# Windowed attention with a feed-forward layer: TensorE in the order of the program, one weight piece per step

## The chip, the cores and the metric

The kernel runs on one core of a Trainium2 chip. The metric is the time of one execution on the device in microseconds (us), the median of several runs. TensorE (PE) multiplies, VectorE (DVE), ScalarE (ACT) and GpSimd (POOL) work on elements, SyncE (SP) issues most of the transfers. PEld is TensorE's loading of the stationary operand.

## What is computed

Eight batches, eight heads, 576 positions of 64 numbers. Four heads attend to the last 32 positions, four to every fourth of the last 128. The result, as 4608 rows of 512, goes through a feed-forward layer with a hidden width of 2048.

```python
    scores = scale * np.matmul(q, k.transpose(0, 1, 3, 2))
    scores = np.where(masks[None, :, :, :], scores, -1000000000.0)
    attn = softmax(scores)                      # written out in the reference
    x = np.matmul(attn, v)  # as (4608, 512)
    h = x @ w_in                                # 512 -> 2048
    g = h * np.clip(h + 3.0, 0.0, 6.0) / 6.0
    out = g @ w_out                             # 2048 -> 512
```

## The kernel before, in words

**Attention.** 48 "trios" `t` hold a sixth of a batch's query blocks each. For a trio `st_both` issues 48 small score matmuls (L163) and, between them, 48 small value matmuls (L173 or L181) of an earlier trio: one block. For the first 12 trios (`NFIRST`) a mask matmul (L228) stands ahead. `softmax` is two DVE operations (L195, L196; three for the later trios) and one exponential on ACT (L200). `normalise` is three on DVE (L207, L208, L210). The first 12 trios are transposed on PE (`turn`, L242; ACT copies the result, L245 for the attention weights `a`, L247 for the output `xf`), the later 36 on DVE with four small transfers (`turn_by_blocks`). `st_split` writes `xf` as a rounded part `xh` (ACT, L299) and a rest `xl` (POOL, L302), the input of the feed-forward layer.

**Feed-forward.** 12 chunks `c` of 384 rows, 16 slices `f` of the hidden width: 192 steps `(c, f)`. `gemm1` of a step is 12 matmuls of 384 columns (L407 to L409); ACT and DVE turn them into `gh` and `gl` (L412, L413, L416, L417); `gemm2`, two steps later (`LAG`), is 9 matmuls of 512 columns (L428 to L430). The order of the steps is (0,0) to (0,3), then (0,4), (1,0), (0,5), (1,1) and so on, then chunk after chunk.

**Weights.** They come in 32 pieces (piece 2f is slice f of `w_in`, piece 2f+1 of `w_out`). `convert_beat` moves each piece through three stages, one stage a beat: `cv_fields` (two ACT operations L338, L339, one DVE L340), `cv_join` (DVE L346, L350, ACT L351), `cv_split` (DVE L355). A beat also issues the loads of pieces up to three ahead (`load_ahead`, on SP). 32 pieces need 34 beats.

**Order.** The start is a loop over `tau` from 0 to 15: `first_items(tau)` traces the block of trio `tau` (scores) and `tau-3` (values), the transpose of the weights of trio `tau-1`, the transpose and split of trio `tau-4`; then come the beats of `CB` (14, two each for tau 6 to 12) and the steps of `EARLY` (step 0 at tau 8, ... step 7 and 8 at tau 15). The other steps follow. `step_at(n)` traces `gemm1` of step n, pieces of attention from `beside`, a beat, `gemm2` of step n-2, more of `beside`, and, for even n from 4 to 28, another beat. The program's order isn't the order of issue: every instruction carries a priority (`turn_of`), and a scheduler orders each engine's queue by priority and by the times that it simulates. `turn_of` gives `first_items(tau)` and `gemm1` of step tau-8 the same number. Within a queue the order is fixed at compile time, and each engine works it off in that order. `pace` ties the loads and two of the ACT operations of a piece behind the last PE instruction traced, in that scheduler's order.

Two PSUM pools matter: `ps_h` (2 buffers, `gemm1`) and `ps_a` (6 buffers: blocks, transposes, and three for the output of each open chunk).

Of the kernel before, what the change touches and what calls it, by code (L numbers as in the profile page):

```python
# [23 lines left out]
SPARE = 2  # L24
WORK = 12
BEATS = 30
EXTRA = 2
WARM = 8
ONV = ()
AHEAD = 3  # L30
LEAD = 4
# [15 lines left out]
def windowed_attention_ffn(ctx: ExitStack, tc: tile.TileContext, qk, vp, w, mask, out):  # L47
# [286 lines left out]
    def cv_fields(p):  # L334
        if p % 2 == 0:
            wt[p // 2] = wpool.tile([P, 4, WN], F32R, name="wt", tag="w")
        hi_w, lo_w, v, a, _, _ = parts(p)
        pace(nc.scalar.mul(v, hi_w, 2.0**-112))  # L338
        pace(nc.scalar.mul(a.bitcast(U32), lo_w.bitcast(U32), 2.0**-29))  # L339
        nc.vector.tensor_scalar(  # L340
            out=v.bitcast(U32), in0=v.bitcast(U32), scalar1=3, scalar2=None, op0=ALU.logical_shift_left
        )

    def cv_join(p):
        hi_w, _, v, a, hi, _ = parts(p)
        nc.vector.scalar_tensor_tensor(  # L346
            out=v.bitcast(U32), in0=hi_w.bitcast(U32), scalar=0x80000000, in1=v.bitcast(U32),
            op0=ALU.bitwise_and, op1=ALU.bitwise_or,
        )
        nc.vector.tensor_tensor(out=v.bitcast(U32), in0=v.bitcast(U32), in1=a.bitcast(U32), op=ALU.add)  # L350
        nc.scalar.copy(hi, v)  # L351

    def cv_split(p):
        _, _, v, _, hi, lo = parts(p)
        nc.vector.tensor_tensor(out=lo, in0=v, in1=hi.bitcast(F32), op=ALU.subtract)  # L355
        del staged[p]
# [5 lines left out]
    def load_ahead(n):  # L362
        while beat["loaded"] < min(n, NP):
            f = beat["fields"] // 2
            if len(staged) + f + 1 + 1 > NF + SPARE and len(staged) > 0 and beat["loaded"] >= 2:
                break
            load_w(beat["loaded"])
            beat["loaded"] += 1

    def convert_beat():  # L370
        if beat["split"] < beat["join"]:
            cv_split(beat["split"])
            beat["split"] += 1
        if beat["join"] < beat["fields"]:
            cv_join(beat["join"])
            beat["join"] += 1
        p = beat["fields"]
        if p < NP:
            load_ahead(p + 1)
            if p < beat["loaded"]:  # L380
                cv_fields(p)
                beat["fields"] += 1
        load_ahead(p + AHEAD)
# [10 lines left out]
    def turn_of(n):  # L394
        tc.cur_priority = max(first[0] + int(n * STEP), 0) + 1000

    def gemm1(n, c, f):
        last["g"] = True
        weights_ready(f)
        assert all(x in written for x in trios if c in chunks(*x))  # L400
        read[c] += 1
        r0 = (c * CH) % (2 * S)
        ph = ps_h.tile([P, CH], F32, name="ps_h")
        for kt in range(NK):
            a, b = xh[:, kt, r0 : r0 + CH], xl[:, kt, r0 : r0 + CH]
            ks = slice(kt * P, (kt + 1) * P)
            nc.tensor.matmul(ph, lhsT=wt[f][:, 0, ks], rhs=a, start=(kt == 0), stop=False)  # L407
            nc.tensor.matmul(ph, lhsT=wt[f][:, 0, ks], rhs=b, start=False, stop=False)  # L408
            last["pe"] = nc.tensor.matmul(ph, lhsT=wt[f][:, 1, ks], rhs=a, start=False, stop=(kt == NK - 1))  # L409
        turn_of(n + EV)  # L410
        t = work_tile("t")
        nc.scalar.activation(t, ph, AF.Relu, bias=three, scale=1.0)  # L412
        nc.vector.scalar_tensor_tensor(out=t, in0=t, scalar=6.0, in1=ph, op0=ALU.min, op1=ALU.mult)  # L413
        gh = work_tile("gh", F32R)
        gl = work_tile("gl", F32R)
        nc.scalar.copy(gh, t)  # L416
        nc.vector.tensor_tensor(out=gl, in0=t, in1=gh.bitcast(F32), op=ALU.subtract)  # L417
        gs[c, f] = gh, gl

    def gemm2(c, f):  # L420
        gh, gl = gs.pop((c, f))
        if f == 0:
            po[c] = [ps_a.tile([P, DM], F32, name="ps_o", tag="ps_a") for _ in range(TT)]
        if f == NF - 1:
            o = wpool.tile([P, TT, DM], F32, name="o", tag="w")
        for tt in range(TT):
            ts = slice(tt * P, (tt + 1) * P)
            nc.tensor.matmul(po[c][tt], lhsT=gh[:, ts], rhs=wt[f][:, 2], start=(f == 0), stop=False)  # L428
            nc.tensor.matmul(po[c][tt], lhsT=gh[:, ts], rhs=wt[f][:, 3], start=False, stop=False)  # L429
            last["pe"] = nc.tensor.matmul(po[c][tt], lhsT=gl[:, ts], rhs=wt[f][:, 2], start=False, stop=(f == NF - 1))  # L430
            if f == NF - 1:
                nc.scalar.mul(o[:, tt], po[c][tt], 1.0 / 6.0)
                r = c * CH + tt * P
                nc.scalar.dma_start(out=out[r : r + P, :], in_=o[:, tt])
# [40 lines left out]
    def step_at(n):  # L475
        c, f = steps[n] if n < len(steps) else (None, None)
        turn_of(n)
        if c is not None:
            gemm1(n, c, f)
        turn_of(n + DEL)  # L480
        for step in beside.get((c, f, 0), []):
            step()
        turn_of(n + 0.4)
        if LEAD <= n < BEATS:
            convert_beat()
        turn_of(n + G2)
        if n >= LAG:
            gemm2(*steps[n - LAG])
        turn_of(n + DEL + 0.5)
        for step in beside.get((c, f, 1), []):  # L490
            step()
        turn_of(n + 0.9)
        if LEAD <= n < BEATS and n % EXTRA == 0:
            convert_beat()

    first[0] = BASE * STEP
    some = P + 2 * CH
# [12 lines left out]
    n = 0  # L510
    for tau in range(NFIRST + 4):
        turn_of(tau - BASE)
        first_items(tau)
        turn_of(tau - BASE + CD)
        for _ in range(CB.count(tau)):
            convert_beat()
        for _ in range(EARLY.count(tau)):
            step_at(n)
            n += 1
    while n < len(steps) + LAG:  # L520
        step_at(n)
        n += 1
# [92 lines left out]
```

## Time and profile before

| | us |
|---|---|
| median of 3 runs (lowest to highest) | 915.77 (915.74 to 917.31) |
| the profiled execution | 915.34 |
| its span | 913.6 |
| PE busy, PEld busy | 891.0, 791.6 |
| DVE, ACT, POOL busy | 444.0, 346.5, 62.5 |

The span is what the profiler sees between the first and the last instruction; 1.74 us of the execution's time lie around it. The page gives busy shares over the whole span and in 40 slices of 22.84 us; a stretch is read with the views by window and in order of time. The end of a matmul is modelled, and matmuls overlap, so what one costs in a sequence is the distance from its start to the start of the next.

### The profile page before, as it was taken

What the parts mean: (1) busy time and instruction counts of PE and PEld (TensorE: products, weight loads), DVE (VectorE), ACT (ScalarE), POOL (GpSimd) and SP (SyncE); (2) the same over time, 40 slices, a digit from 0 to 9 for tenths busy, and PEclk for the clock granted to TensorE, in tenths of its full rate; (3) what the DMA queues carried; (4) which work ended last, traced back from release to release, by engine and by line L of the source; (5) the groups of instructions that cost most, each with busy time, mean ns of one, the idle gap of its engine ahead of it and who ended that gap; (6) DMA issues with size and microseconds to landing.
All of it is one profiled execution on the core that took longest, in us unless ns stands there. A gap on an engine that the chain in (4) does not pass through costs nothing.

```text
span 913.6 us, 20574 instructions
## 1 busy us (share of the span) xinstructions
PE 891.0 (98%) x8732; PEld 791.6 (87%) x8732; DVE 444.0 (49%) x934; ACT 346.5 (38%) x661; POOL 62.5 (7%) x77
## 2 busy tenths in 40 slices
PE   6897999999999999999999999999999999999998
PEld 4576999989889899899888989988888998899996
DVE  3899983244545454444454445445444544422221
ACT  2778862333333333233333223233333332332322
POOL 0212100000010110000000000000100010000000
PEclk9799999999999999999999999999999999999999
DMA  9927430022313222222122123113211310100000
GB/s 354 386 83 260 140 93 0 1 95 89 86 54 119 72 70 81 66 67 84 47 85 85 48 64 104 51 46 99 71 49 52 116 32 11 45 5 1 36 1 34
DMA packets 37820, 74.87 MB, mean 82 GB/s; under 512 B 7264, under 2 KB 16608, under 8 KB 37728
## 3 DMA queue, kind: packets, MB, share of 16 engines
q1 hardware_dynamic: 32544, 64.12, 21.8%
q10 hardware_dynamic: 5184, 9.44, 2.7%
q8 instruction: 68, 1.11, 0.5%
q14 instruction: 24, 0.20, 0.1%
HBM read 57.02 MB, written 9.44 MB: 73 GB/s over the span
## 4 chain that ended last, share of the span: by engine, by line
PE 92%; DMA 4%; DVE 2%; ACT 1%; issue 0%; SPq 0%; POOL 0%
PE ps_o L428 15%; PE ps_h L407 15%; PE ps_h L409 14%; PE ps_h L408 14%; PE ps_o L429 14%; PE ps_o L430 14%; PE ps_a L181 3%; PE ps_a L163 2%; DMA first<-in_v 2%; DMA st<-in_w 1%; DMA v<-in_v 1%; DVE st L350 1%; DVE st L346 1%; DVE wt L355 0%; PE ps_a L242 0%
## 5 line engine op out<-in xcount | busy, mean ns | idle before, releaser
L413 DVE SCALAR_TENSOR_TENSOR t<-t,ps_h 128x384 f32<-128x384 f32 x192 | 106.3, 554 | 326.0 <-ACT t L412 325.8
L407 PE MATMUL ps_h<-xh,wt 128*128 128x384 f32 x768 | 261.5, 341 | 2.9 <-DVE t L413 2.8
L408 PE MATMUL ps_h<-xl,wt 128*128 128x384 f32 x768 | 259.9, 338 | 0.5 <-POOL xl L302 0.5
L409 PE MATMUL ps_h<-xh,wt 128*128 128x384 f32 x768 | 259.9, 338 | 0.0
L428 PE MATMUL ps_o<-wt,gh 128*128 128x512 f32 x576 | 228.7, 397 | 2.0 <-ACT gh L416 2.0
L429 PE MATMUL ps_o<-wt,gh 128*128 128x512 f32 x576 | 224.9, 390 | 0.0
L430 PE MATMUL ps_o<-wt,gl 128*128 128x512 f32 x576 | 221.3, 391 | 0.6 <-DVE gl L417 0.6
L412 ACT ACTIVATE t<-ps_h,three 128x384 f32<-128x384 f32 x192 | 111.1, 579 | 273.3 <-PE ps_h L409 273.0
L417 DVE TENSOR_TENSOR gl<-t,gh 128x384 fp32r<-128x384 f32 x192 | 107.0, 557 | 101.4 <-ACT gh L416 100.1
L407 PEld LDWEIGHTS ps_h<-xh,wt 128*128 128x128 f32 x768 | 144.9, 189 | 11.8 <-DVE t L413 3.3
L408 PEld LDWEIGHTS ps_h<-xl,wt 128*128 128x128 f32 x768 | 144.9, 189 | 8.7 <-POOL xl L302 0.6
L409 PEld LDWEIGHTS ps_h<-xh,wt 128*128 128x128 f32 x768 | 145.0, 189 | 0.8 <-issue 0.3
L416 ACT CAST gh<-t 128x384 fp32r<-128x384 f32 x192 | 98.5, 513 | 111.3 <-DVE t L413 109.1
L430 PEld LDWEIGHTS ps_o<-wt,gl 128*128 128x128 f32 x576 | 108.2, 188 | 24.2 <-DVE gl L417 1.0
L428 PEld LDWEIGHTS ps_o<-wt,gh 128*128 128x128 f32 x576 | 108.3, 188 | 20.1 <-ACT gh L416 2.3
L429 PEld LDWEIGHTS ps_o<-wt,gh 128*128 128x128 f32 x576 | 108.4, 188 | 15.7
L302 POOL TENSOR_TENSOR xl<-xf,xh 128x384 fp32r<-128x384 f32 (+3 forms) x72 | 62.2, 877 | 740.6 <-ACT xh L299 671.8
L200 ACT ACTIVATE e<-e 128x384 f32<-128x384 f32 x48 | 25.2, 526 | 112.4 <-DVE e L196 112.3
L163 PE MATMUL ps_a<-kq 64*32 64x64 f32 x1872 | 47.1, 225 | 0.0
L299 ACT CAST xh<-xf 128x384 fp32r<-128x384 f32 (+3 forms) x72 | 33.7, 536 | 34.7 <-DMA xf<-xf_t 34.6
L181 PEld LDWEIGHTS ps_a<-v,a 64*32 64x32 f32 x1728 | 35.8, 105 | 9.2 <-issue 8.6
L181 PE MATMUL ps_a<-v,a 64*32 64x65 f32 x1728 | 41.6, 225 | 0.0
(45 smaller groups left out, 494.6 us busy)
## 6 DMA issues: line engine op xcount, KB each, us to landing
st<-in_w SPq DMA_DIRECT2D x32, 512.0 KB, 5.7
kq<-in_qk SPq DMA_DIRECT2D x39, 416.0 KB, 4.5
v<-in_v SPq DMA_DIRECT2D x39, 390.0 KB, 3.5
out<-o ACTq DMA_DIRECT2D x36, 256.0 KB, 2.9
first<-in_qk SPq DMA_DIRECT2D x9, 416.0 KB, 8.0
first<-in_v SPq DMA_DIRECT2D x9, 390.0 KB, 8.5
a<-a_t SPq DMA_DIRECT2D x144, 24.0 KB, 1.8
xf<-xf_t SPq DMA_DIRECT2D x144, 24.0 KB, 1.8
```

The costliest lines, as they stand in the source:

```text
L163: last["pe"] = nc.tensor.matmul(ps[at : at + QB, 2 * QB * i : 2 * QB * (i + 1)], lhsT=x[rows, KW + QB * n : KW + QB * (n + 1)], rhs=x[rows ...
L181: last["pe"] = nc.tensor.matmul(ps[at : at + QB, i * W : (i + 1) * W], lhsT=ats[t][rows, QB * n : QB * (n + 1)], rhs=vs[t][rows, n, :], st ...
L407: nc.tensor.matmul(ph, lhsT=wt[f][:, 0, ks], rhs=a, start=(kt == 0), stop=False)
L408: nc.tensor.matmul(ph, lhsT=wt[f][:, 0, ks], rhs=b, start=False, stop=False)
L409: last["pe"] = nc.tensor.matmul(ph, lhsT=wt[f][:, 1, ks], rhs=a, start=False, stop=(kt == NK - 1))
L412: nc.scalar.activation(t, ph, AF.Relu, bias=three, scale=1.0)
L413: nc.vector.scalar_tensor_tensor(out=t, in0=t, scalar=6.0, in1=ph, op0=ALU.min, op1=ALU.mult)
L416: nc.scalar.copy(gh, t)
L417: nc.vector.tensor_tensor(out=gl, in0=t, in1=gh.bitcast(F32), op=ALU.subtract)
L428: nc.tensor.matmul(po[c][tt], lhsT=gh[:, ts], rhs=wt[f][:, 2], start=(f == 0), stop=False)
L429: nc.tensor.matmul(po[c][tt], lhsT=gh[:, ts], rhs=wt[f][:, 3], start=False, stop=False)
L430: last["pe"] = nc.tensor.matmul(po[c][tt], lhsT=gl[:, ts], rhs=wt[f][:, 2], start=False, stop=(f == NF - 1))
```

## The change

TensorE's queue is taken out of the scheduler's hands: within `manual_schedule` its instructions stay in the order in which the program traces them. A block of `st_both` is then issued whole, the transposes follow it, and the step's `gemm1` and `gemm2` come after them. The queues of the other engines are ordered as before. The second beat of the even steps goes (13 of 53 beats that could run; 34 do work), so from step 4 on one piece moves on per step.

```diff
-EXTRA = 2
...
         for step in beside.get((c, f, 1), []):
             step()
         turn_of(n + 0.9)
-        if LEAD <= n < BEATS and n % EXTRA == 0:
-            convert_beat()
...
     with tile.TileContext(nc, schedule_with_timeline_sim=True) as tc:
-        windowed_attention_ffn(tc, *args, o)
+        with tc.manual_schedule(engines={mybir.EngineType.PE}):
+            windowed_attention_ffn(tc, *args, o)
```

## Rows read from the trace of the kernel before

**Rows 1.** The page: busy us, share of the span and instructions of each engine.
```profile
PE 891.0 (98%) x8732; PEld 791.6 (87%) x8732; DVE 444.0 (49%) x934; ACT 346.5 (38%) x661; POOL 62.5 (7%) x77
```

**Rows 2.** By stretch: us; PE, PEld, DVE, ACT, POOL busy (instructions); PE clock, DMA share, GB/s.
```profile
34.19:66.03 31.84, 31.23 (x476) 22.43 (x475) 29.11 (x58) 24.03 (x49) 6.44 (x7) 0.86 0.49 178
66.03:95.48 29.45, 24.10 (x246) 20.11 (x245) 29.05 (x59) 24.70 (x51) 7.59 (x7) 0.94 0.73 254
95.48:127.00 31.52, 31.52 (x163) 28.93 (x162) 31.45 (x61) 25.34 (x49) 1.31 (x1) 1.00 0.38 117
127.00:904.77 777.77, 777.77 (x7164) 701.39 (x7162) 338.33 (x725) 256.21 (x484) 43.08 (x54) 1.00 0.19 57
```

**Rows 3.** PE in order of time (start, us): a plain step, one with a block inside gemm1.
```profile
310.18 0.34 PE L407 MATMUL ps_h<-xh,wt 128*128 128x384 f32 x1
...
312.27 0.39 PE L428 MATMUL ps_o<-wt,gh 128*128 128x512 f32 x1
...
314.31 0.34 PE L407 MATMUL ps_h<-xh,wt 128*128 128x384 f32 x1
...
319.74 0.34 PE L407 MATMUL ps_h<-xh,wt 128*128 128x384 f32 x1
```

**Rows 4.** PE in order of time: a step with its block between gemm1 and gemm2.
```profile
328.00 0.34 PE L407 MATMUL ps_h<-xh,wt 128*128 128x384 f32 x1
...
333.47 0.34 PE L407 MATMUL ps_h<-xh,wt 128*128 128x384 f32 x1
```

**Rows 5.** PE in order of time: values of a first trio alone, then transposes.
```profile
70.68 0.94 PE L173 MATMUL ps_a<-v,a 64*32 64x65 f32 x48
71.56 0.55 PE L242 MATMUL ps_a<-ident,e 128*128 128x128 f32 x3
71.94 0.49 PE L242 MATMUL ps_a<-ident,x 128*128 128x128 f32 x3
```

**Rows 6.** PE in order of time: step 0, alternating with a block of trio 8.
```profile
34.19 0.78 PE L407 MATMUL ps_h<-xh,wt 128*128 128x384 f32 x1
...
35.24 0.69 PE L408 MATMUL ps_h<-xl,wt 128*128 128x384 f32 x1
```

**Rows 7.** PE in order of time, 79 to 93 us, waits in brackets.
```profile
79.63 0.55 PE L242 MATMUL ps_a<-ident,x 128*128 128x128 f32 x3
...
82.82 0.34 PE L409 MATMUL ps_h<-xh,wt 128*128 128x384 f32 x1
...
90.00 0.44 PE L407 MATMUL ps_h<-xh,wt 128*128 128x384 f32 x1 [2.82 <-DVE t L413]
...
91.84 0.53 PE L409 MATMUL ps_h<-xh,wt 128*128 128x384 f32 x1
92.16 0.53 PE L407 MATMUL ps_h<-xh,wt 128*128 128x384 f32 x1
```

**Rows 8.** DVE in order of time: the last pieces ahead of step 4.
```profile
64.42 1.28 DVE L355 TENSOR_TENSOR wt<-st,wt 128x512 fp32r<-128x512 f32 x2
```

**Rows 9.** DVE groups, 27 to 95.48 us: busy us, mean ns, idle before and releaser.
```profile
L355 DVE TENSOR_TENSOR wt<-st,wt 128x512 fp32r<-128x512 f32 x18 | 13.9, 776 | 1.4 <-ACT wt L351 1.4
```

**Rows 10.** DVE in order of time, without idle time: six operations from 123.25 to 126.33 us.
```profile
123.25 0.42 DVE L340 TENSOR_SCALAR st<-st 128x512 uint32<-128x512 uint32 x1
...
124.19 0.55 DVE L417 TENSOR_TENSOR gl<-t,gh 128x384 fp32r<-128x384 f32 x1
124.66 0.68 DVE L346 SCALAR_TENSOR_TENSOR st<-st 128x512 uint32<-128x512 uint32 x1
...
126.33 0.68 DVE L350 CUSTOM_DVE_ANT_0 st<-st 128x1024 uint16<-128x1024 uint16 x1
```

**Rows 11.** ACT in order of time, 83 to 88 us.
```profile
83.06 0.91 ACT L299 CAST xh<-xf 128x96 fp32r<-128x96 f32 x2
...
87.34 0.56 ACT L412 ACTIVATE t<-ps_h,three 128x384 f32<-128x384 f32 x1
```

**Rows 12.** POOL in order of time: the last part of chunk 1's input.
```profile
83.51 2.15 POOL L302 TENSOR_TENSOR xl<-xf,xh 128x96 fp32r<-128x96 f32 x2 [0.95 <-ACT xh L299]
```

## What the change will do

> **What bounds the kernel now.** I read the page first, then the stretches, then single engines in order of time. The page says that PE is busy for 98% of the span and DVE for 49% [rows 1]; taken as one number that leaves 22.6 us to gain, anywhere. The stretches say where [rows 2]: from 127 us to the end PE is busy for 777.77 of 777.77 us with DVE at 338, and already from 95.48 to 127 us it is busy for all of 31.52 us although DVE has no room left (31.45). So from 95.48 us, where `gemm1` of step 8 starts, the end is fixed by the PE work that is left; only what moves that start moves the end.
>
> A plain step costs 4.13 us there, 2.09 for `gemm1` and 2.04 for `gemm2` [rows 3]. A step with an attention block inside its `gemm1` takes 5.43 us, so the block costs 1.30; with the block between `gemm1` and `gemm2` it takes 5.47, so 1.34 [rows 3, 4].
>
> Before 95.48 us I count what PE had to do at the full clock, by starts: a block 1.30, its mask like a matmul of 384 columns 0.17 [rows 3], values alone 0.88, a transpose (three matmuls) 0.38 [rows 5]. From 34.19 to 66.03 us: four blocks, three of them with mask (5.7), seven transposes (2.7), `gemm1` of steps 0 to 3 (8.4), `gemm2` of 0 and 1 (4.1): 20.9 of 31.84 us, 10.9 lost. From 66.03 to 95.48 us: `gemm1` of steps 4 to 7 (8.4), `gemm2` of 2 to 4 and two thirds of 5 (7.5), three times values (2.6), six transposes (2.3): 20.8 of 29.45 us, 8.65 lost. Together 19.6 us.
>
> The busy time of PE alone would give 0.6 and 5.35 us for the two [rows 2], because slow work counts as busy. The loads of weights leave 9.4 and 9.3 us [rows 2], near my 10.9 and 8.65. The Trainium skill, page Trainium Kernel Development and Optimization, section Performance Expectations, says that matmul busy time is a bad measure of the distance to the roofline and the share of weight loads a good one. By the first the whole stretch has 6 us to give, by the second 18.7; the trace agrees with the second.
>
> Why it is lost: DVE is busy for 29.11 of 31.84 and 29.05 of 29.45 us [rows 2]; it carries softmax, the conversion of weights and the activation. And PE changes between a 128x128 matmul and two small ones: such an exchange takes 1.05 us at the low clock [rows 6], where matmuls in a row start 0.32 us apart [rows 7].
>
> **The change part by part.**
>
> *Up to 34 us.* Block, transposes, next block already follow each other as traced. I take nothing; two mask matmuls change places, worth at most their 0.17 us each, either way.
>
> *Steps 0 to 3 (34 to 66 us).* The 16 single matmuls of `gemm1` that alternate with pairs of small ones go together. An exchange is 1.05 us against some 0.37 (a matmul at 0.32 and two small ones), so six at the low clock lose some 4 us, and the ten at the full clock, at half of that, 3 [rows 6, 7]. But this stands beside a DVE with 2.7 us free [rows 2], and `gemm1` of step 4 starts 0.3 us after DVE has split the pieces it waits for (65.70 us) [rows 8]. The beats up to there (14, from `CB`) aren't touched. Bounds 0 and 2.7 us; I take 0, as the row of DVE is nearest.
>
> *The second beat.* Up to `gemm1` of step 8 two extra beats have run (steps 4 and 6). DVE agrees: 18 pieces were split by 95.48 us [rows 9], and 14+4 beats alone would have split 16. `gemm1` of step 8 (slice 6) needs piece 12. The six DVE operations from 123.25 to 126.33 us are one piece's four and one step's two, 3.08 us; the step's two are 0.47 each, so a beat is 2.14 [rows 10]. Two beats are 4.3 us of DVE in a stretch where it has 0.4 us free [rows 2]. Each also takes three ACT operations, with ACT busy for 24.70 of 29.45 us, and a load of 512 KB on SP; moved later, these let the loads of trios 12 to 14 go ahead in SP's queue, for which nobody waits so early. POOL's queue is not passed. The beats dropped from step 8 on lie where PE is busy throughout [rows 2]: nothing, and without that cover they would give back only what PE waits for DVE there, which is 0.
>
> *A wait that goes.* PE waits 2.82 us for a `ps_h` buffer that `t` (L413) holds [rows 7]. That activation started on ACT at 87.34 us [rows 11], behind operations of two pieces, for a `gemm1` whose last matmul started at 82.82 [rows 7]. Fewer beats shorten that queue.
>
> *New waits.* In program order `gemm1` of step 5 (chunk 1) directly follows the transpose of trio 9, and its second half needs `xl` of that trio. Behind it in PE's queue stand `gemm2` of step 3 and the values of trio 11, and DVE waits for these. In the trace the chain runs from 79.63 us (transpose) over ACT to 85.66 (end of L302): 6.0 us, much of it in ACT's queue [rows 7, 11, 12]. Without the queue it is a copy of some 0.5 us on ACT, 0.91 and 2.15: 3.6 us [rows 11, 12]. PE has half a `gemm1` (1.04 us) beside it, so it idles for 2.6 to 5.0 us; I take 2.6, as ACT has less to do after the change. The same stands at step 0 behind trio 4, where DVE is the bound: nothing. And of the six `ps_a` buffers three hold the output from step 2 on, so a transpose may wait for the copy of the one before, between nothing and 1 us a tau; I take 1 us in all, as PE shows no such wait now.
>
> *After step 8.* DVE then needs 3.08 of 4.13 us a step [rows 3, 10]. `gemm1` of an even step n needs the `w_in` piece split four steps earlier, 16 us. Blocks at odd places move behind `gemm2`: 1.30 against 1.34 us [rows 3, 4], some ten blocks, 0.4 us at most either way. Nothing.
>
> *Sum.* PE's way: 66.03+20.8+2.6+1.0 = 90.4 us for the start of `gemm1` of step 8, 95.48 now: 5.1 us earlier. DVE's way: 4.3 us less work, 91.2. The two ends lie together; I take 5 us. Against the profiled execution's own 915.34 that is 910.3; the median of the runs is 0.43 us above it, so **910.8 us**.
>
> **The rivals.**
>
> *A, nothing moves (915.5).* The two extra beats are only work done early, and their place in DVE's queue is taken by others; PE's order was near the program's already. For it: DVE stays the busiest engine to 91 us. Against it: the 2.82 us wait behind pieces that nobody needs yet [rows 7, 11].
>
> *B, all of it comes back (905.5).* The 8.65 us lost from 66 us on go, and 1.6 of the 2.7 us that DVE has free before: 915.8-8.65-1.6. For it: DVE then has room for every activation at once. Against it: the new wait at step 5. B's 1.6 us is what is left of DVE's room after a wait of 1 us.
>
> *C, slower (919.6): the order holds PE up.* The chains behind trios 4 and 9 cost 5 us each with ACT's queue, the `ps_a` buffers 1 us in each of three taus, and half of the 20.8 us runs at the low clock, where matmuls start 0.32 us apart instead of 2.09/12 = 0.17 [rows 3, 7] (+10.4). Then PE needs 41.7+13+10.4 = 65.1 us for what took 61.3: 4 us more, 919.6. It decides where waits and slow clock pass the 19.6 us lost now. For it: the rows show the clock at 0.86 and 0.94 in both stretches [rows 2]. Against it: blocks in one piece leave fewer changes of tile shape. The Trainium skill, page TensorE: Matmul & The Clock Gate, section Why this matters for your kernels, warns of idle gaps between bursts of matmuls, after which the clock is halved: by that rule a PE that may not fill a wait with other work should lose; no row here shows yet how long the new waits are.
>
> **How the numbers follow.** Forecast (907 to 913.9) 0.58, A 0.13, B 0.11, C 0.18. About 0.2% is what a measurement of this kernel can tell from no change, so faster means below 913.9 and slower above 917.6. Faster: 0.58+0.11 = 0.69; same: A, 0.13; slower: C, 0.18. The range runs from B's time to 917.5, which leaves out half of B's case at the lower end and most of C.
>
> **What the profile after would show.** Right: whole `gemm1` and blocks between 34 and 66 us; `gemm1` of step 8 near 90.4 us and PE without a gap from there; 16 pieces split at that time; DVE with idle time between 95 and 127 us; splits that go on to some 150 us. One gap of 2.6 us before the second half of step 5. The steady steps unchanged at 4.13 us and blocks at 1.3. Wrong: step 4 later than 66 us (then the order holds DVE up), gaps after step 8 at `gemm1` for weights, or a clock well under 0.9 between 34 and 90 us.

## The result, and the profile after

| | before | after |
|---|---|---|
| median of 20 runs (us) | 915.89 | 917.37 |
| lowest to highest | 912.98 to 917.42 | 915.82 to 919.31 |
| the profiled execution, its span | 915.34, 913.6 | 916.58, 914.8 |

The ratio is 1.0018, with a 95% interval of 1.0010 to 1.0025: the changed kernel is 1.5 us slower by the medians (1.6 by the ratio), just under the 0.2% that the prediction called no change, though the interval reaches past it. The forecast was 910.8, faster. Executions of one kernel differ by up to 4.4 us here (912.98 to 917.42 before), and a profile shows one of them, so a difference of a microsecond between two profiles is weak evidence. All names of lines are one lower after the change, since a constant above them went.

The same stretches as in [rows 2], from the changed kernel (us; PE, PEld, DVE, ACT, POOL busy; PE clock, DMA share, GB/s):

```profile
34.19:66.03 31.84, 22.42 (x455) 18.48 (x453) 29.78 (x63) 25.10 (x51) 7.53 (x6) 0.75 0.58 207
66.03:95.48 29.45, 27.14 (x256) 23.25 (x257) 25.83 (x49) 21.27 (x43) 8.48 (x8) 0.88 0.53 184
95.48:127.00 31.52, 31.52 (x161) 28.70 (x161) 24.81 (x46) 20.52 (x39) 1.14 (x1) 1.00 0.37 123
127.00:904.77 777.77, 776.95 (x7164) 701.07 (x7163) 348.97 (x741) 261.31 (x496) 43.05 (x54) 1.00 0.19 59
```

In the first stretch PE loads weights for 18.48 us instead of 22.43, at a clock of 0.75 instead of 0.86: it falls behind. In the second it loads for 23.25 instead of 20.11: it catches up. From 95.48 us on little differs but DVE, which is no longer full (24.81 instead of 31.45). So the question lies ahead of 95 us. These lines of PE's list of waits (engine, line, releaser; us in all, times, longest) show what is new:

```profile
PE ps_h L406 <- ACT xh L298: 4.6, 2, 3.0
PE ps_a L241 <- ACT a L244: 3.9, 1, 3.9
PE ps_h L407 <- POOL xl L301: 1.3, 2, 0.7
PE ps_a L180 <- DMA a<-a_t: 0.8, 1, 0.8
```

None of the first two was there before, and the waits for `t`, `gh` and `gl`, as the 2.82 us in [rows 7], are gone. In order of time PE shows where (start, duration, idle before in brackets):

```profile
61.75 0.55 PE L241 MATMUL ps_a<-ident,e 128*128 128x128 f32 x3
66.15 0.55 PE L241 MATMUL ps_a<-ident,x 128*128 128x128 f32 x3 [3.86 <-ACT a L244]
...
69.06 0.52 PE L407 MATMUL ps_h<-xl,wt 128*128 128x384 f32 x1
69.38 0.52 PE L408 MATMUL ps_h<-xh,wt 128*128 128x384 f32 x1
...
73.87 0.42 PE L406 MATMUL ps_h<-xh,wt 128*128 128x384 f32 x1
...
79.06 0.55 PE L241 MATMUL ps_a<-ident,x 128*128 128x128 f32 x3
79.37 0.42 PE L406 MATMUL ps_h<-xh,wt 128*128 128x384 f32 x1
...
82.23 0.45 PE L406 MATMUL ps_h<-xh,wt 128*128 128x384 f32 x1 [1.57 <-ACT xh L298]
83.30 0.44 PE L407 MATMUL ps_h<-xl,wt 128*128 128x384 f32 x1 [0.62 <-POOL xl L301]
...
84.29 0.51 PE L427 MATMUL ps_o<-wt,gh 128*128 128x512 f32 x1
...
88.03 0.28 PE L172 MATMUL ps_a<-v,a 64*32 64x65 f32 x4
```

The transpose of trio 7 at 66.15 us waited 3.86 us for a `ps_a` buffer, which the copy of trio 10's attention weights on ACT had to set free. At 69.06 to 69.38 us matmuls start 0.32 us apart: the low clock. `gemm1` of step 4 starts at 73.87 instead of 66.03 us (two of the 7.8 us are values and transposes that program order puts ahead of it). `gemm1` of step 5 starts at 79.37 and takes 4.92 us instead of 2.09, and the `gemm2` behind it 3.74 instead of 2.04, again at the low clock.

PE's waits are one side of the 7.8 us. The other is what DVE did ahead of step 4. The first two lines below count the pieces that were split by then, before (to 66.03 us) and after (to 73.87); the third is the stretch from 34.19 us to step 4 after the change, for which [rows 2] has 31.84 us with DVE busy for 29.11 (columns as there):

```profile
L355 DVE TENSOR_TENSOR wt<-st,wt 128x512 fp32r<-128x512 f32 x10 | 7.6, 768 | 1.4 <-ACT wt L351 1.4
L354 DVE TENSOR_TENSOR wt<-st,wt 128x512 fp32r<-128x512 f32 x12 | 9.3, 779 | 0.8 <-ACT wt L350 0.7
34.19:73.87 39.68, 30.14 (x533) 25.33 (x532) 36.91 (x76) 30.33 (x62) 11.00 (x8) 0.75 0.51 184
```

DVE splits 12 pieces instead of 10. It is busy for 7.8 us more of a stretch that is 7.8 us longer, and has 2.8 us without work, as before (2.7). The chain of work that ended last, as the profile infers it, agrees: before, from 50 us to step 4, it lies on PE; after, from 51.06 to 69.64 us, it lies nearly all on DVE, and 63% of it on the four lines that convert weights (L339, L345, L349, L354):

```profile
by line: PE ps_a L163 13.8%; PE ps_h L409 13.4%; PE ps_h L407 12.2%; PE ps_a L242 11.7%; PE ps_a L173 11.1%; PE ps_h L408 11.0%; PE ps_o L428 8.6%; PE ps_o L430 8.6%; PE ps_o L429 8.5%; PE ps_a L228 2.1%
by line: DVE st L349 23.7%; DVE st L345 20.2%; DVE wt L354 12.9%; DVE x L209 7.6%; DVE e L195 7.5%; DVE st L339 6.1%; DVE gl L416 5.0%; DVE t L412 5.0%; DVE mx L194 4.5%; issue 3.8%; ACT wt L350 3.4%; DVE z L206 1.6%; DVE z L207 1.6%; DVEq 
```

What counts in the end is the start of step 9, where before and after have the same work behind them:

| start of `gemm1` (us) | step 4 | step 9 | step 9 to the last matmul |
|---|---|---|---|
| before | 66.03 | 100.29 | 808.3 |
| after | 73.87 | 102.00 | 808.7 |

1.7 us are lost ahead of step 9 and 0.4 behind it (0.8 us is one wait of a block for the small transfers of `turn_by_blocks`, in the list above). The two profiled executions differ by 1.2 us: 0.8 are won back between the end of the last matmul and the end of the span, which take 3.7 us in all eight kernels with PE in program order and 4.6 us in the six others.

### The profile page after: what moved, and what is told of

Same layout as the page of the kernel before. It is cut to its first block, busy times and chain, and to the rows that moved or that the text cites. A ratio compares the mean times of both kernels' runs of the same rounds, so it can differ in the third digit from the quotient of the medians.

```text
span 914.8 us, 20569 instructions
## 1 busy us (share of the span) xinstructions
PE 887.2 (97%) x8732; PEld 792.6 (87%) x8732; DVE 446.7 (49%) x934; ACT 346.4 (38%) x661; POOL 64.4 (7%) x77
## 4 chain that ended last, share of the span: by engine, by line
PE 90%; DVE 3%; DMA 3%; ACT 2%; issue 1%; SPq 0%; POOL 0%; DVEq 0%
PE ps_o L427 15%; PE ps_h L406 14%; PE ps_h L407 14%; PE ps_h L408 14%; PE ps_o L428 14%; PE ps_o L429 14%; PE ps_a L180 3%; PE ps_a L162 2%; DMA first<-in_qk 1%; DMA st<-in_w 1%; DVE st L349 1%; DVE st L345 1%; DVE wt L354 1%; DMA kq<-in_qk 1%; ACT st L337 0%
## 5 line engine op out<-in xcount | busy, mean ns | idle before, releaser
L429 PE MATMUL ps_o<-wt,gl 128*128 128x512 f32 x576 | 225.2, 391 | 0.0
L301 POOL TENSOR_TENSOR xl<-xf,xh 128x384 fp32r<-128x384 f32 (+3 forms) x72 | 64.1, 903 | 740.8 <-ACT xh L298 725.2
```

## The experiments

Ratios are to the kernel before, timed on the same chip, with 95% intervals; gains and losses in us are mostly taken from them. "Step 9" is the start of its `gemm1` in that run's profile.

**The two halves of the change by themselves.** The first kernel takes PE's order alone:

```diff
+        with tc.manual_schedule(engines={mybir.EngineType.PE}):
+            windowed_attention_ffn(tc, *args, o)
```

> The kernel before with the program's order on PE alone; the second beats stay. Theory Q (queue): PE in program order waits behind copies and casts that stand late in ACT's queue, and the second beats cost nothing: the same as the changed kernel, 917.4 us within 0.8, with a wait of several us before a transpose near 62 us. Theory D (DVE bounds the start, and two beats are 4.3 us of it, as the prediction had it): the beats come on top of the order's cost, 920 to 922 us.

919.24 us, ratio 1.0031 (1.0020 to 1.0041), step 9 at 104.14. The order alone costs 2.8 us, more than the whole change and between the figures of the two theories; the wait for the copy on ACT is there, 3.9 us. The second takes away the second beats alone:

```diff
-        if LEAD <= n < BEATS and n % EXTRA == 0:
-            convert_beat()
```

> The kernel before without the second beats; PE's queue is ordered by the scheduler as before. Theory Q: 915.9 us within 0.8, since DVE splits as many pieces before step 8 whatever the program allows. Theory D: 4.3 us less, 911.6 us, and gemm1 of step 8 near 91 us instead of 95.5.

914.59 us, ratio 0.9977 (0.9966 to 0.9987), step 9 at 97.64. Taking the beats away gains 2.1 us, half of what I had reckoned, and again neither theory's figure. The halves add up, within their intervals, to the whole (1.0008 against 1.0018). So both parts of the sum were wrong in size, and the order also in sign.

Where do 2.1 us come from, if not from DVE doing 4.3 us less? DVE split 17 pieces before step 8 there (92.83 us), against 18 before (95.48), and was busy for 70.88 us up to it instead of 73.79. So less than two pieces went, but DVE's 2.9 us would be enough for the gain. PE shows another way to it. Clock by stretch, first before, then without the second beats (columns as above):

```profile
88.00:92.00 4.00, 2.00 (x9) 2.01 (x10) 4.00 (x9) 3.69 (x8) 0.00 (x0) 0.88 1.03 411
92.00:96.00 4.00, 4.00 (x17) 3.60 (x16) 3.97 (x8) 2.75 (x7) 1.54 (x1) 0.69 0.72 227
```
```profile
88.00:92.00 4.00, 3.09 (x18) 2.97 (x19) 3.75 (x8) 3.41 (x7) 0.09 (x1) 1.00 1.01 388
92.00:96.00 4.00, 4.00 (x22) 3.67 (x21) 3.83 (x7) 3.55 (x8) 1.17 (x2) 1.00 0.83 335
```

Before, PE waited 2.82 us for `t` [rows 7], and the clock then fell to 0.69 of full. Without the beats `t` came earlier on DVE and the clock stayed at 1.00 (first before, then without them, DVE in order of time):

```profile
88.19 0.68 DVE L355 TENSOR_TENSOR wt<-st,wt 128x512 fp32r<-128x512 f32 x1
88.79 0.68 DVE L346 SCALAR_TENSOR_TENSOR st<-st 128x512 uint32<-128x512 uint32 x1
89.39 0.55 DVE L413 SCALAR_TENSOR_TENSOR t<-t,ps_h 128x384 f32<-128x384 f32 x1
```
```profile
87.71 0.69 DVE L349 CUSTOM_DVE_ANT_0 st<-st 128x1024 uint16<-128x1024 uint16 x1
88.31 0.55 DVE L412 SCALAR_TENSOR_TENSOR t<-t,ps_h 128x384 f32<-128x384 f32 x1
```

That is 1.1 us at the wait; nine matmuls and what follows at 0.32 instead of 0.17 us give about the other 1.5 of the 2.65 us in these two profiles. If the gain hangs on one operation's place, more beats needn't cost more:

```diff
-EXTRA = 2
+EXTRA = 1
```

> The kernel before with a second beat at every step from 4 on instead of every even one, so four extra beats before step 8 instead of two. Theory L (each extra beat before step 8 costs half of its 2.14 us of DVE, as taking two away gave 2.1 us): 2.1 us more than before, 917.5 to 919 us. Theory N (the extra beats cost only where they delay one certain operation): no change, within 0.8 us of before.

915.97 us, ratio 1.0000 (0.9988 to 1.0012). But this run doesn't decide it, since DVE did no more work. Up to step 8 (97.63 us) it split the same 18 pieces and was busy for 74.11 us, against 73.79:

```profile
L355 DVE TENSOR_TENSOR wt<-st,wt 128x512 fp32r<-128x512 f32 x18 | 14.3, 800 | 1.4 <-ACT wt L351 1.4
```

Beats that the program allows earlier aren't work that DVE does earlier. Whether the 2.1 us are DVE's amount of work or the place of one operation stays open.

**The gap behind trio 9.** Steps 5 and 6 change places, so that `gemm1` of chunk 0 stands where PE waited:

```diff
+    steps[5], steps[6] = steps[6], steps[5]
     beside = {}
```

> The changed kernel with steps 5 and 6 exchanged, so that gemm1 of slice 5 for chunk 0 stands between the transpose of trio 9 and gemm1 of chunk 1. Theory Q: the gap of 2.9 us inside gemm1 of chunk 1 goes, and with it the slow clock after it (1.7 us in the gemm2 that follows): 912.8 to 915 us. Theory D: DVE's load is the same, so 917.4 within 0.8, the wait only moves.

914.07 us, ratio 0.9977 (0.9966 to 0.9987), 3.75 us under the changed kernel. Step 9 at 98.72. PE has no gap there (the new step 5 between 80.42 and 82.59):

```profile
80.42 0.42 PE L406 MATMUL ps_h<-xh,wt 128*128 128x384 f32 x1
...
82.41 0.34 PE L408 MATMUL ps_h<-xh,wt 128*128 128x384 f32 x1
82.59 0.39 PE L427 MATMUL ps_o<-wt,gh 128*128 128x512 f32 x1
```

I had expected the exchange to do nothing where the scheduler orders PE, since it already put step 6 into the gap. So the same without the order, first on the kernel before:

> The kernel before with steps 5 and 6 exchanged and nothing else. If the late input of chunk 1 costs the scheduler's order the same 2.8 us as it did without the second beats: 913 us, ratio 0.997. If DVE's second beats bound that stretch, the exchange has nothing to gain: 915.8 within 0.8.

914.06 us, ratio 0.9981 (0.9969 to 0.9993): 1.6 us gained, with all beats in place. And together with the beats:

> The kernel before without the second beats and with steps 5 and 6 exchanged; PE's queue is ordered by the scheduler. Theory G: the scheduler already puts the other step into the gap, so the exchange does nothing: 914.6 us as without it, within 0.8. Otherwise, if the late input of chunk 1 also costs time there, 911.5 to 913.5 us.

911.80 us, ratio 0.9955 (0.9943 to 0.9968), step 9 at 95.79. Theory G falls here: the late input of chunk 1 costs the scheduler's order too. What the scheduler did was to start step 5, go on with step 6 and finish step 5 later; then both `ps_h` buffers were held, step 6's activation stood behind step 5's on ACT, and step 7 waited. That is the 2.82 us in [rows 7]. The exchange alone leaves 1.3 us of waits for `t`, in two pieces; with the beats gone too, PE's list of waits has no line for `ps_h` from DVE:

```profile
PE ps_o L427 <- ACT gh L415: 1.0, 1, 1.0
PE ps_a L241 <- DVE x L209: 0.6, 1, 0.6
PE ps_a L241 <- ACT e L199: 0.5, 2, 0.3
PE ps_h L407 <- POOL xl L301: 0.5, 1, 0.5
```

With the exchange on both sides, program order still costs 0.9977 against 0.9955, 2.0 us. What it loses, it loses before step 4 (74.94 against 66.46 us, two of them work moved ahead), and the next runs ask how.

**The waits before step 4.** All of these contain the exchange, except the first. In the changed kernel seven operations ran on ACT between the transpose at 61.75 us and the copy that PE waited for:

```profile
61.95 0.62 ACT L350 CAST wt<-st 128x512 fp32r<-128x512 f32 x1 [1.28 <-DVE st L349]
62.47 0.66 ACT L337 ACTIVATE st<-st 128x512 f32<-128x512 f32 x1
63.04 0.66 ACT L338 ACTIVATE st<-st 128x512 uint32<-128x512 uint32 x1
63.59 0.65 ACT L337 ACTIVATE st<-st 128x512 f32<-128x512 f32 x1
64.15 0.49 ACT L415 CAST gh<-t 128x384 fp32r<-128x384 f32 x1
64.55 0.67 ACT L338 ACTIVATE st<-st 128x512 uint32<-128x512 uint32 x1
65.12 0.61 ACT L350 CAST wt<-st 128x512 fp32r<-128x512 f32 x1
65.62 0.47 ACT L244 COPY a<-ps_a 128x384 f32<-128x384 f32 x1
```

Six of them belong to pieces of weights. The first attempt puts the pieces' ACT operations behind the copies traced before them, by order edges (`behind_copy` adds one to the copy last traced):

```diff
-        pace(nc.scalar.mul(v, hi_w, 2.0**-112))
-        pace(nc.scalar.mul(a.bitcast(U32), lo_w.bitcast(U32), 2.0**-29))
+        pace(behind_copy(nc.scalar.mul(v, hi_w, 2.0**-112)))
+        pace(behind_copy(nc.scalar.mul(a.bitcast(U32), lo_w.bitcast(U32), 2.0**-29)))
...
-        nc.scalar.copy(hi, v)
+        behind_copy(nc.scalar.copy(hi, v))
```

> The changed kernel; in addition the three ACT operations of a weight piece stand behind the last transposed copy traced (an order edge on ACT's own queue, no work added). Theory Q: the 3.9 us wait of the transpose at 62 us for the copy of trio 10 falls under 1 us, and the waits of gemm1 of step 0 for xh shrink by 1 to 3 us; gemm1 of step 8 starts 3 to 6 us earlier than the changed kernel's 97.9, time 911.5 to 914.5 us. Theory D: ACT's pieces come later, DVE with them, and as DVE bounds the start the time stays at 917.4 or grows.

920.64 us, ratio 1.0045 (1.0030 to 1.0059): slower by 2.5 us than the changed kernel. The wait became 2.9 us and step 4 started at 72.29, 1.6 us earlier; but `gemm1` of step 5 then took 8.93 us, since trio 9's copy stood behind other pieces and behind a cast that waited for DVE. A miss for theory Q in the form I gave it. With the exchange as well:

> The changed kernel with steps 5 and 6 exchanged, and with the ACT operations of a weight piece behind the last transposed copy traced. Theory G (gap): the order on PE costs only the gap behind trio 9, which the exchange covers; other waits of PE before step 8 stand beside DVE's work: the same as the exchange alone, 914.1 us within 0.8. Theory S (sum): every wait of PE before step 8 counts; the edge took 1.6 us off the wait at 62 us, so 912.5 us.

914.24 us, ratio 0.9986 (0.9975 to 0.9996): no better than the exchange alone. Its step 4 starts at 74.89, as there (74.94), although DVE had split 10 pieces by then and not 12: the wait for the copy fell from 3.5 to 2.8 us, and another transpose waited 1.6 us for a cast on ACT. Next, the transposes moved away from the wait:

```diff
+    LATE = (10, 11, 12)
...
+        if tau not in LATE:
+            turn_x_items(tau)
...
         for _ in range(EARLY.count(tau)):
             step_at(n)
             n += 1
+        if tau in LATE:
+            turn_of(tau - BASE)
+            turn_x_items(tau)
```

> The changed kernel with steps 5 and 6 exchanged, and at tau 10 to 12 the transpose of the trio's output traced behind the step instead of ahead of it, so that gemm1 and gemm2 stand between the two transposes and cover the wait for a ps_a buffer. The wait of 3.5 us near 64 us should be gone in the trace. Theory G: 914.1 us within 0.8. Theory S: 2 to 3.5 us less, 910.5 to 912 us.

915.36 us, ratio 0.9995 (0.9985 to 1.0004). The wait wasn't gone. It went to the other transpose and to another copy, still for a `ps_a` buffer:

```profile
67.13 0.90 PE L241 MATMUL ps_a<-ident,e 128*128 128x128 f32 x3 [4.07 <-ACT xf L246]
```

Step 0 one tau later, behind the block of trio 9:

```diff
-EARLY = (8, 9, 10, 11, 12, 13, 14, 15, 15)
+EARLY = (9, 9, 10, 11, 12, 13, 14, 15, 15)
```

> The changed kernel with steps 5 and 6 exchanged, and step 0 traced at tau 9 beside step 1, so that the block of trio 9 stands between the transpose of trio 4 and gemm1 of step 0. The waits of 3.1 and 0.7 us inside gemm1 of step 0 should be gone. Theory G: 914.1 us within 0.8. Theory S: 3 to 4 us less, 910 to 911 us.

914.30 us, ratio 0.9981 (0.9971 to 0.9991), the exchange's own 0.9977 within the intervals. `gemm1` of step 0 took 3.5 us instead of 8.4, its waits were gone, and step 4 started at 74.37 instead of 74.94 all the same. Those waits were covered, as the prediction had said. This run and the one with the edges on ACT speak against theory S, by which every wait of PE counts. Last, less conversion ahead of step 4:

```diff
-CB = (6, 6, 7, 7, 8, 8, 9, 9, 10, 10, 11, 11, 12, 12)
+CB = (6, 6, 7, 7, 8, 8, 9, 10, 10, 11, 12, 12, 13)
```

> The changed kernel with steps 5 and 6 exchanged, and with four beats of the start later: 6, 7, 9, 10, 12 and 13 beats by tau 8 to 13 instead of 6, 8, 10, 12, 14, so that two pieces less are converted before step 4. In that kernel PE runs at full pace from step 4 on, and step 4 starts at 74.9 us. Theory D (DVE and ACT, full of conversion, bound the start of step 4 and make the waits for buffers long): step 4 starts 2 to 4.3 us earlier, 910 to 912 us against 914.1. Theory P (PE's own waits in program order bound it): step 4 stays at 74 to 75 us, 914.1 within 0.8; later weights could only add.

911.01 us, ratio 0.9951 (0.9935 to 0.9968), 4.7 us under the kernel before. Step 4 starts at 71.12, 3.8 us earlier, as theory D had it, and step 9 at 96.19. DVE has split 10 pieces ahead of step 4 and is busy for 32.27 us from 34.19 us on, instead of 12 and 37.95 us with the exchange alone. Three operations of pieces stand ahead of the copy on ACT instead of six, and PE waits 1.49 us:

```profile
62.43 0.51 ACT L415 CAST gh<-t 128x384 fp32r<-128x384 f32 x1 [1.01 <-DVE t L412]
62.84 0.68 ACT L337 ACTIVATE st<-st 128x512 f32<-128x512 f32 x1
63.44 0.60 ACT L350 CAST wt<-st 128x512 fp32r<-128x512 f32 x1
63.94 0.65 ACT L338 ACTIVATE st<-st 128x512 uint32<-128x512 uint32 x1
64.50 0.45 ACT L244 COPY a<-ps_a 128x384 f32<-128x384 f32 x1
```
```profile
65.01 0.55 PE L241 MATMUL ps_a<-ident,x 128*128 128x128 f32 x3 [1.49 <-ACT a L244]
65.31 0.42 PE L406 MATMUL ps_h<-xh,wt 128*128 128x384 f32 x1
```

`gemm1` of step 3 then ran at the full clock (2.17 us, against 3.24 in the changed kernel). Is that good for the scheduler's order too?

> The kernel before without the second beats, with steps 5 and 6 exchanged and the same four beats later; PE's queue is ordered by the scheduler. Theory D: 1 to 4 us less than without the later beats (911.8), 908 to 911 us. Theory P, or weights that come too late for steps 3 and 4: 911.8 within 0.8 or more.

916.23 us, ratio 1.0009 (0.9994 to 1.0024): 4.4 us more than without it. There PE waits 2.8 us for `gh` at 73 to 76 us, and step 9 starts at 100.98. Why the later pieces hurt the scheduler's order stays open.

## Why the prediction was wrong, point by point

**What bounds the kernel.** Right. From step 9 to the last matmul all thirteen other kernels and the kernel before take 807.9 to 809.3 us, and the time of the profiled execution follows the start of step 9: 100.29 and 915.3 us before, 95.79 and 910.9 without the second beats and with the exchange, 96.19 and 911.1 for program order with less conversion ahead. Where PE's order is the program's, this part is up to 1.0 us longer than before's 808.3.

**Up to 34 us, after step 8, blocks at odd places.** Right: nothing, but for the one wait of 0.8 us and the 0.8 us won back behind the last matmul, which the forecast didn't have.

**Steps 0 to 3: taken at 0, bounds 0 and 2.7 us of gain.** This is the step that failed. I bounded it from one side only, as if program order could but leave PE's waits where DVE covers them, and took DVE's work up to step 4 as given ("the beats aren't touched"). Step 4 came 7.8 us later, 5.8 without the two us of other work ahead of it. DVE stayed as full as it was, but it had two more pieces to split by then, 12 instead of 10: before, the scheduler had started step 4 ahead of the last two.

Along PE the same 5.8 us can be counted as a wait that stood in the sum, under new waits, with 1 us in all for the `ps_a` buffers. It was 3.86 us, and the low clock behind it made `gemm1` of step 3 take 3.24 and `gemm2` of step 1 2.67 us, 1.8 us over the full clock's 2.09 and 2.04. I priced that wait by the duration of the copy (0.5 us) and not by what stands ahead of the copy in ACT's queue, six operations of pieces, though I had done just that for trio 9. But the wait by itself isn't the price. With the exchange, moving the transposes, the pieces on ACT or step 0 left step 4 at 74.4 to 75.9 us, against 74.94 (without the exchange the edges on ACT brought 1.6 us, which went again behind trio 9). Taking two pieces out from ahead of step 4 moved it to 71.12. So the runs show the conversion ahead of step 4 in place of the 0. How much of it acts through DVE's amount of work and how much through ACT's queue, no run separates; the count of pieces alone isn't it, as the run with the exchange and the edges also had 10 by then.

**The second beat: 4.3 us.** Mis-sized. It measured 2.1 us in the scheduler's order, 2.4 with the exchange, 1.2 in program order (1.0031 to 1.0018, whose intervals touch). In the changed kernel 18 pieces were split by the start of step 8, as before, and not the 16 of the forecast, and DVE was busy for 73.49 us up to it against 73.79: taking beats out of the program left as much on DVE there as before, and one piece less than the order alone (19). I counted beats in the program's order, while DVE's queue is still ordered by the scheduler. In the scheduler's order one piece less was split, `t` came 1.1 us earlier at one wait, and the clock didn't fall after it; which of these is the price stays open.

**The wait that goes.** The 2.82 us went, but my reading was wrong. The activation at 87.34 us [rows 11] wasn't behind pieces: the last matmul of step 5 ran until about 87.2. It was step 5's activation; step 6's, whose `gemm1` ended at 83, stood behind it. From its end it was 1.5 us to `t` on DVE, behind two operations of pieces. The exchange of steps alone leaves 1.3 us of this wait, without any room added on ACT.

**The gap at step 5: 2.6 us.** Right: 4.92-2.09 = 2.8. But PE's low clock behind it (3.74 against 2.04 us for `gemm2`) adds 1.7, which I had left out of the forecast and had in rival C only.

**The rivals.** C had part of the mechanism: waits in program order and the slow clock behind them. Its price was too high by 2.2 us; only one of its two chains counted (the other, behind trio 4, was covered, as the forecast said), and it had nothing of the pieces ahead of step 4. The Trainium skill's warning (page TensorE: Matmul & The Clock Gate, section Why this matters for your kernels) agrees with the trace as far as the clock fell: 0.75 and 0.88 in the two stretches, against 0.86 and 0.94. It fell behind shorter waits than the page has in view, too, and not behind all (last section).

**The sum.** Forecast, to step 9: -5. Measured: +5.8 before step 4, and from step 4 to step 9 28.1 us plus the two us of work moved ahead of it, against 34.3: -4.1. That the second part came out near the forecast is partly luck: the two pieces that DVE had split ahead of step 4 were no longer to be split behind it (6 up to step 8, instead of 8), and the forecast had them as beats that go. The first part I had set to nothing.

## What to carry to other kernels

An engine put into program order can no longer fill a wait with other work. So price a wait for a buffer by the queue of the engine that sets it free, not by that engine's operation, and bound a step that is "covered" from both sides. When another engine is full, count what the new order puts ahead of the point that matters: here two pieces more on DVE and ACT ahead of step 4. When input arrives late, give the next step to somebody else at the level of the program; here that was worth 1.6 us in the scheduler's order and 3.75 in program order. With the exchange and less conversion ahead program order comes to 911.0 us; the best of the scheduler's order, 911.8, can't be told from it (ratios 0.9951 and 0.9955, with intervals that nearly coincide).

## What the runs showed of the hardware that I had not expected

PE's clock fell after short waits. In the changed kernel PE waited 1.57 and 0.62 us between 80 and 84 us, at a clock of 1.00. Over the next four us the clock was at 0.57, mostly the lower of its two levels, and matmuls of 512 columns started 0.43 us apart instead of 0.23.

```profile
80.00:84.00 4.00, 1.81 (x9) 1.23 (x8) 3.81 (x9) 3.02 (x7) 1.51 (x2) 1.00 0.92 309
84.00:88.00 4.00, 4.00 (x12) 2.80 (x10) 2.67 (x5) 2.86 (x5) 0.00 (x0) 0.57 0.14 53
```

After the 1.89 us that PE waited for `t` without the second beats, where before it waited 2.82, the clock didn't fall, nor after the 1.49 us with less conversion ahead. So the waits of 2.2 and 3.86 us in the changed kernel cost 1.7 and 1.8 us more behind them, and two shorter ones cost nothing more.
